# GpSimd's fills for the paired heads wait for step 24 instead of step 16, and the planner gets one weight instead of five

## The chip, the cores and the metric

The kernel runs on one core of a Trainium2 chip. The metric is the device time of one execution in microseconds, as a median over runs of the same program on the same chip. The profile shows one execution, taken by the hardware profiler.

The engines are named as in the profile: PE is the matrix engine (TensorE), PEld its weight loads, DVE is VectorE, ACT is ScalarE, POOL is GpSimd and SP is SyncE, which here issues nearly all of the DMAs. SPq, POOLq and the like are the sequencers of these engines.

## The reference

A causal attention with a decay runs over 4 batches, 8 heads, 576 positions and heads of 64. Its output, 2304 tokens by 512, goes through two MLPs (512 to 2048 to 512), the first with a squared ReLU, the second with a piecewise quadratic:

```python
scores = q @ k.T / sqrt(D) + cum[:, None] - cum[None, :]   # cum: running sum of log(clip(f))
attn = softmax(where(causal, -1e9, scores)); x = attn @ v  # per head, then heads side by side
h = x @ moe_w_in;   g = relu(h) ** 2;                               x = g @ moe_w_out
h = x @ moe2_w_in;  g = where(h >= 1, h, where(h <= -1, 0, (h + 1) ** 2 / 4));  out = g @ moe2_w_out
```

The weights are float64, the other inputs float32; the kernel computes each product of the MLPs as three float16 matmuls (high times high, low times high, high times low).

## The kernel before, in words

The tokens are cut into four blocks: blocks 0 to 2 have 512 columns each, the last one has 768. For each of the first three blocks the two MLPs run as 16 steps each (steps 0 to 15 of block 0's first MLP, 16 to 31 of its second MLP, 32 to 47 of block 1's first MLP, and so on). A step `s` has three parts: `h_group(s)` multiplies one 128-wide slice of the first weight matrix into a bank `h` (L1423 on PE, 12 matmuls); `act_group(s)` makes the activation `g` from it and splits it into a high half `gh` and a rest `gl` (in the second MLP L1451 and L1453 on ACT, L1455 on DVE, then L741 or L745 for `gh` and L758 for `gl`); `out_group(s)` multiplies `gh` and `gl` into the four accumulators `acc` (L1587 to L1589, 12 matmuls). `out_group(s)` follows one step behind, after `h_group(s + 2)`. The weights come in as float64 words (`raw`), are decoded (L1332, L1335 or L1336, L1340 or L1341, L1343), split (L1398 or L1399, L758) and stored for later use (L1405).

Attention is computed beside this: for positions below 256 in groups of four heads (`attention32`, tiles with a q in their name, such as `s6q`), and for the later positions in pairs of heads (`attention_pair`), first for block 2. The pairs need tiles that are partly constant: `Q1`, `Q2`, `K1`, `K2` (two of each, with zeros and with rows of plus or minus a constant), a wider `mask`, and a mask `pairs` for two heads at once. These constants are written once by POOL: `rows_of_pairs` makes 10 fills of Q tiles and 4 of K tiles (L668), one fill and one select for the mask (L653, L654), and one fill and two selects for `pairs` (L676, L678). All of them wait for one tiny POOL operation, the gate `gated<-x` (L662). In the kernel before it reads the last slice of `x2b[0]`, the input of block 0's second MLP, and the call is made at step 17.

After the fills, SP copies the decay rows into the tiles (`K<-cumhl`, `Q<-cumhl`, L1118), ACT and DVE write the heads' halves, and PE makes the first scores of a pair (L1141, L1142).

The order of all instructions on all engines is written out by a planner in the kernel file (`Schedule`). Every operation has a due time and a cost estimate, and where two engines can do it, one for each. `run` makes a list schedule and puts such an operation on the engine with the earliest weighted end, `(1 + weight) * cost` after its start, with weights for DVE and POOL and none for ACT. `improve` does that in seven rounds for each of the weights in `WEIGHTS`, with due times taken back from the round before, and keeps the plan that its own estimate finds shortest. In the planner, POOL and those DVE operations that are marked as sharing SBUF's port with it (a third entry in their cost) never overlap. Of the five weights of the kernel before, the plan that it runs is one of weight 0.6 for DVE and 0.3 for POOL.

Of the kernel before, what the change touches and what calls it, by code (L numbers as in the profile page):

```python
# [17 lines left out]
ALU = mybir.AluOpType  # L18
# [5 lines left out]
NKC = DM // P  # L24
NFC = DFF // P
# [41 lines left out]
def pattern(bits):  # L67
    return struct.unpack("f", struct.pack("I", bits))[0]
# [62 lines left out]
TURN = 0.05  # L131
LEAD = 15.4

WEIGHTS = [{"DVE": x, "POOL": x / 2} for x in (0.4, 0.5, 0.6, 0.8, 1.0)]

class Buf:
    def __init__(self, pool, make, kind=None):
# [25 lines left out]
class Schedule:  # L163
# [175 lines left out]
    def improve(self, pools, rounds):  # L339
        first = [o.due for o in self.ops]  # L340
        best = None
        for weight in WEIGHTS:
            for o, f in zip(self.ops, first):
# [71 lines left out]
def tile_attention_moe_moe(ctx: ExitStack, tc: tile.TileContext, qkv, f, w2, outT, halves, seen=None, bad=None):  # L415
# [19 lines left out]
    sch = Schedule()  # L435
# [111 lines left out]
    V = [T_START]  # L547
# [28 lines left out]
    gated = const.tile([1, 1], F16, name="gated")  # L576
# [13 lines left out]
    def setup():  # L590
# [3 lines left out]
        due = -100.0  # L594
        G, V_, A = nc.gpsimd, nc.vector, nc.scalar
# [56 lines left out]
        def triangle(a, z, due, deps=()):  # L652
            m1 = sch.op(due, {"POOL": ((z - a) / 1200 + 0.05, lambda: G.memset(mask[:, a:z], 0.0))}, deps)  # L653
            ms.append(sch.op(due, {"POOL": ((z - a) / 940 + 0.2, lambda: G.affine_select(  # L654
                out=mask[:, a:z], in_=mask[:, a:z], pattern=[[-1, z - a]], compare_op=ALU.is_ge,
                fill=-BIG, base=OFF - a, channel_multiplier=1))}, [m1]))
# [2 lines left out]

        def rows_of_pairs(due, x, ops):  # L660

            z = sch.op(due, {"POOL": (0.1, lambda: G.tensor_scalar(gated, x.tile[:1, 0, 1, :1], 1.0, None, op0=ALU.mult))}, ops, [x])  # L662
            gate = [z]
            for i in range(2):
                def fill(t, r, c, x, z):
                    bits = {0.0: 0, SQ: 0x78007800, -SQ: 0xF800F800}[x]
                    n = t[0:r, :, c].shape[2]
                    return sch.op(due, {"POOL": (n / 900 + 0.1, lambda: G.memset(t[0:r, :, c].bitcast(F32), pattern(bits)))}, [z])  # L668

                every, left, right = slice(0, None), slice(0, D), slice(D, None)  # L670
                z = fill(Q2[i], D, right, 0.0, gate[0])
                z = fill(Q2[i], 6, right, SQ, z)
                zs["Q", i] = [fill(Q1[i], P, left, 0.0, gate[0]), fill(Q2[i], P, left, 0.0, gate[0]), fill(Q2[i], 3, right, -SQ, z)]
                zs["K", i] = [fill(K2[i], 6, every, SQ, fill(K2[i], D, every, 0.0, gate[0]))]
            triangle(0, OFF + P - HEAD, due, gate)
            m1 = sch.op(due, {"POOL": (0.4, lambda: G.memset(pairs, 0.0))}, gate)  # L676
            for a in range(2):
                ms.append(sch.op(due, {"POOL": (0.5, lambda a=a: G.affine_select(  # L678
                    out=pairs[D * a:D * a + D, :], in_=pairs[D * a:D * a + D, :], pattern=[[-1, HEAD + D]],
                    compare_op=ALU.is_ge, fill=-BIG, base=HEAD, channel_multiplier=1))}, [m1]))  # L680

        if not halves:
            due = -30.0
            triangle(0, OFF + P - HEAD, 60)
            for i in range(2):
                for n, t in (("Q", Q2[i]), ("K", K2[i])):
                    z = None
                    for r, x in ((64, 0.0), (4, -1.0 if n == "Q" else 1.0)):
                        z = sch.op(due, {"POOL": (0.5, lambda t=t, r=r, x=x: G.memset(t[0:r, :].bitcast(F32), x))}, [z])
# [10 lines left out]
    cum_op, zs, mask_op, id_op, cumd_op, first_rows, rows_of_pairs = setup()  # L700
# [583 lines left out]
    def w_load(s):  # L1284

        if s >= NS:
            return
        first, again = {}, {}
        for layer, u in ((0, s + LAG), (1, s)):
            if 0 <= u < NS:  # L1290
                _, mo, fc = steps[u]
                pair = mo * NFC + (fc - LAG * (layer == 0)) % NFC
                (again if (pair, layer) in scr_op else first).setdefault(pair, []).append(layer)
        ops = whl_op[s] = []
        if first:
            b = new("raw" if halves else "big", f"raw{s}", [P, 2, 512], U64) if W64 else new("wf", f"wf{s}")
            loads = []
            for pair, layers in first.items():
                c = span(layers)
                size = P * (8 if W64 else 4) * 512 * len(layers)  # L1300
                loads.append(sch.op(V0(s + 2) - 17, {
                    "SP": (dma_t(size, late=2.5 if s < 0 else 0.0), lambda b=b, c=c, pair=pair: nc.sync.dma_start(
                        out=b.tile[:, c], in_=w2[pair].rearrange("p (l n) -> p l n", l=2)[:, c]))},
                    [], [b], early=RE[s + LAG] if s <= 0 else V0(s + 2) - 17 - LW))
                for layer in layers:
                    scr_op[pair, layer] = None
            raw[s] = b, loads
            new_pairs[s] = first
        if again:
            b = whl[s] = new("big", f"whl{s}")  # L1310
            for pair, layers in again.items():
                c = span(layers)
                ops.append(sch.op(V0(s + 2) - 7, {
                    "SP": (dma_t(P * 1024 * NB * len(layers), late=1.2), lambda b=b, c=c, pair=pair: nc.sync.dma_start(
                        out=wide(b.tile[:, c]), in_=scr[pair][:, c]))},
                    [scr_op[pair, layer] for layer in layers], [b]))
# [67 lines left out]
    def w_split(s):  # L1384

        if s not in wf:
            return
        c = span(sorted(layer for layers in new_pairs[s].values() for layer in layers))
        n = 512 * (c.stop - c.start)
        w = wf.pop(s)  # L1390
        if s not in whl:
            whl[s] = new("big", f"whl{s}")
        b = whl[s]
        due = V0(s + 2) - 4.5
        hi, lo = (lambda i=i: b.tile[:, c, i, :] for i in range(2))
        src, unit = lambda: w.tile[:, c], sw * (2.0 if W64 and not halves else 1.0)
        o = sch.op(due, {
            "ACT": (act_t(n), lambda: nc.scalar.activation(hi(), src(), AF.Copy, scale=unit)),  # L1398
            "DVE": (dve2_t(n), lambda: nc.vector.tensor_scalar(hi(), src(), unit, None, op0=ALU.mult), True),  # L1399
        }, whl_op[s], [w, b])  # L1400
        o = sch.op(due + 1, subs(lo, src, lambda: wide(hi()), n, scale=unit, seen=mark("w")), [o], [w, b])
        whl_op[s].append(o)
        for pair, layers in new_pairs[s].items():
            c_ = span(layers)
            store = sch.op(due + 6, {"SP": (dma_t(P * 1024 * NB * len(layers)), lambda c_=c_, pair=pair: nc.sync.dma_start(  # L1405
                out=scr[pair][:, c_], in_=wide(b.tile[:, c_])))}, [o], [b])
            for layer in layers:
                scr_op[pair, layer] = store


    h_op, gt, accs, acc_op, x2b, x2_op = {}, {}, {}, {}, {}, {}
# [210 lines left out]
    def attend(blk):  # L1622
        if blk:
            xb[blk] = new_x(f"x{blk}", blk)
        for g in groups:
            if g.blk == blk:
                attention32(g)
        if blk in carry:
            buf, (_, off, c0, c1), deps = carry[blk]
            n = c1 - c0  # L1630
            split_x(blk, range(NKC), off, lambda: buf.tile[:, :, :n], n, deps, buf, V[NFC * ATTENTION[blk][0]] + 2)
        for t in tasks:
            if t.blk == blk:
                (attention_pair if halves else attention)(t)
# [488 lines left out]
    for s in range(NS + LAG):  # L2123
        if s < NS:
            blk, mo, fc = steps[s]
            if halves and s == NFC + 1:
                rows_of_pairs(V[s] + 12, x2b[0], [x2_op[0, NKC - 1]])
            for b, (g, _) in ATTENTION.items():
                if s == NFC * g:
                    attend(b)  # L2130
            w_load(s + LAG)
            w_split(s)
            after = s >= NFC and steps[s - fc - 1] == (blk, 0, NFC - 1)
            if after and fc == 0:
                out_group(s - 2, V[s] - 3)
                out_group(s - 1, V[s] - 2)
            if not halved(s):
                h_group(s)
            elif fc % 2 == 0:
                pair_group(s)  # L2140
            w_decode(s + 1)
            in_sums(s)
            if not halved(s):
                act_group(s)
            if halves and blk in HALVED and fc == 1:
                half_sums(s)
        if s >= LAG and not (s < NS and after and fc < LAG):
            out_group(s - LAG, (V[s] + V[s + 1]) / 2)
# [86 lines left out]
```

## Time and profile before

| what | value |
|---|---|
| median of 3 runs | 863.54 us (862.9 to 866.13) |
| the profiled execution, its own time | 864.67 us |
| its span, first to last instruction | 862.8 us |
| PE busy | 845.9 us (98%) |
| DVE busy | 763.6 us (89%) |
| ACT busy | 605.3 us (70%) |
| POOL busy | 23.8 us (3%) |
| mean granted PE clock | 0.998 |

Busy time is time in which an engine has an instruction in work; a 128x512 matmul of float16 is shown with 0.38 us, but the next one starts 0.21 to 0.22 us after it, so that they overlap. What PE loses is read from the idle time that the timeline shows in brackets ahead of an instruction, together with what ended it.

### The profile page before, as it was taken

The numbers are of one execution on the slowest core, as the hardware profiler recorded it, in microseconds if no ns is written. First come the engines' busy times: TensorE is split into PE (matmuls) and PEld (weight loads), VectorE is DVE, ScalarE is ACT, GpSimd is POOL, SyncE is SP. The second block draws the span as 40 slices with busy tenths as digits, with TensorE's granted clock in tenths as the row PEclk, the third lists the DMA queues.
The fourth block names the chain that finished last, engine by engine and source line by source line (L and its number), as shares of the span: only waits on it lengthen the run. The fifth ranks groups of instructions, "written<-read, shape, count | busy, mean of one in ns | idle before, by whom it ended". The sixth has DMA issues, their size and how long they took to land.

```text
span 862.8 us, 14696 instructions
## 1 busy us (share of the span) xinstructions
PE 845.9 (98%) x4930; PEld 462.7 (54%) x4930; DVE 763.6 (89%) x1882; ACT 605.3 (70%) x1232; POOL 23.8 (3%) x120
## 2 busy tenths in 40 slices
PE   8999999999999999999999999999999999999996
PEld 7644444454444444444446654466556556665553
DVE  8999999999789878989888789986899998999993
ACT  7999988996677667767577577756564566756652
POOL 3000004000000000000000000000000000000000
PEclk9999999999999999999999999999999999999999
DMA  8799997886599998699489988677464454335432
GB/s 258 210 319 323 353 346 230 275 279 222 164 270 226 255 218 241 150 229 257 164 227 264 256 237 208 158 191 161 129 198 156 159 171 159 109 112 168 139 112 76
DMA packets 144841, 180.68 MB, mean 209 GB/s; under 512 B 91670, under 2 KB 96918, under 8 KB 140726
## 3 DMA queue, kind: packets, MB, share of 16 engines
q1 hardware_dynamic: 144750, 179.67, 71.2%
q8 instruction: 40, 0.66, 0.3%
q14 instruction: 43, 0.35, 0.1%
q10 hardware_dynamic: 8, 0.00, 0.0%
HBM read 127.84 MB, written 30.81 MB: 184 GB/s over the span
## 4 chain that ended last, share of the span: by engine, by line
PE 76%; DVE 12%; ACT 6%; DMA 3%; issue 2%; SPq 0%; POOL 0%; DVEq 0%; POOLq 0%; ACTq 0%
PE h L1423 17%; PE acc L1587 8%; PE acc L1589 8%; PE acc L1588 8%; PE h L1972 6%; PE av L1246 3%; PE X L1837 3%; PE Y L1837 2%; PE b L1924 2%; PE b L1926 2%; PE b L1925 2%; DVE wf L1343 2%; PE s L1147 1%; PE s L1146 1%; DMA PT<-PP 1%
## 5 line engine op out<-in xcount | busy, mean ns | idle before, releaser
L1423 PE MATMUL h<-x,whl 128*128 128x512 f16 x912 | 214.3, 379 | 1.0 <-DVE g L1455 1.0
L1423 PEld LDWEIGHTS <-whl 128*128 128x128 f16 x912 | 88.0, 98 | 103.5 <-issue 3.9
L1587 PE MATMUL acc<-gh,whl 128*128 128x512 f16 x312 | 118.3, 379 | 0.0
L1589 PE MATMUL acc<-gl,whl 128*128 128x512 f16 x312 | 118.2, 379 | 0.0
L1588 PE MATMUL acc<-gh,whl 128*128 128x512 f16 x312 | 118.2, 379 | 0.0
L1188 ACT ACTIVATE E<-E,st 128x448 f32<-128x448 f32 (+2 forms) x80 | 54.6, 682 | 33.2 <-DVE st L1186 17.7
L1222 DVE SCALAR_TENSOR_TENSOR PP<-E,st,PP 128x512 f16<-128x512 f32 (+2 forms) x112 | 62.0, 594 | 3.5 <-ACT PP L1218 3.1
L1218 ACT ACTIVATE PP<-E,st 128x512 f16<-128x512 f32 (+2 forms) x112 | 59.4, 588 | 5.9 <-issue 3.5
L1589 PEld LDWEIGHTS <-whl 128*128 128x128 f16 x384 | 37.6, 98 | 45.3
L758 DVE SCALAR_TENSOR_TENSOR gl<-g,gh 128x512 f16<-128x512 f32 x78 | 53.4, 686 | 8.1 <-PE acc L1589 3.2
L1587 PEld LDWEIGHTS <-whl 128*128 128x128 f16 x384 | 37.6, 98 | 40.0 <-issue 3.6
L1588 PEld LDWEIGHTS <-whl 128*128 128x128 f16 x384 | 37.6, 98 | 37.2
L764 DVE CUSTOM_DVE_ANT_0 E<-s,mask 128x288 f32<-128x288 f32 (+1 forms) x96 | 45.4, 509 | 12.1 <-PE s L1147 11.5
L1972 PEld LDWEIGHTS <-wi 128*128 128x128 f16 x336 | 32.9, 98 | 22.8 <-issue 0.9
L1451 ACT ACTIVATE r<-h,half 128x512 f32<-128x512 f32 x40 | 27.1, 678 | 23.6 <-PE h L1423 23.6
L1343 DVE SCALAR_TENSOR_TENSOR wf<-wf,low 128x1024 int32<-128x1024 int32 (+1 forms) x32 | 37.9, 1185 | 2.7 <-ACT low L1340 1.4
L758 DVE SCALAR_TENSOR_TENSOR whl<-wf,whl 128x1024 f16<-128x1024 f32 (+1 forms) x32 | 38.2, 1193 | 1.5 <-ACT whl L1398 1.4
L1332 ACT ACTIVATE wf<-raw 128x1024 f32<-128x1024 f32 (+1 forms) x32 | 35.8, 1119 | 2.0 <-DVE whl L758 1.9
L1641 DVE TENSOR_TENSOR G<-G 128x384 f32<-128x384 f32 x64 | 34.5, 552 | 0.8 <-ACT G L1988 0.4
L1972 PE MATMUL h<-x_last,wi 128*128 128x384 f16 x192 | 33.6, 326 | 0.7 <-DVE G L1996 0.7
L1441 ACT ACTIVATE r<-h 128x512 f32<-128x512 f32 x38 | 22.4, 589 | 13.5 <-PE h L1423 13.1
L1455 DVE SCALAR_TENSOR_TENSOR g<-r,h 128x512 f32<-128x512 f32 x40 | 27.2, 682 | 3.4 <-ACT r L1453 3.1
(620 smaller groups left out, 1924.8 us busy)
## 6 DMA issues: line engine op xcount, KB each, us to landing
raw<-in_w_dram SPq DMA_DIRECT2D x28, 1024.0 KB
whl<-scr SPq DMA_DIRECT2D x56, 512.0 KB
scr<-whl SPq DMA_DIRECT2D x28, 512.0 KB
wo<-scr SPq DMA_DIRECT2D x48, 256.0 KB
k<-in_qkv_dram SPq DMA_DIRECT2D x16, 576.0 KB
wi<-scr SPq DMA_DIRECT2D x23, 256.0 KB
q<-in_qkv_dram SPq DMA_DIRECT2D x16, 320.0 KB
v<-in_qkv_dram SPq DMA_DIRECT2D x16, 320.0 KB
```

Source lines behind the costliest of these rows:

```text
L758: nc.vector.scalar_tensor_tensor(out(), a(), scale, b(), op0=ALU.mult, op1=ALU.subtract, **kw)
L764: return nc.vector.tensor_tensor_reduce(out=out, in0=ps, in1=pairs[:, :n] if q0 is None else mask[:m, OFF - q0:OFF - q0 + n], scale=scale, ...
L1188: o_e.append(sch.op(dc + 0.5, {"ACT": (act_t(e, ptr=1) + 0.14, lambda a=a, e=e, at=at, Ec=Ec: nc.scalar.activation(Ec.tile[:, :e], Ec.tile ...
L1218: nc.scalar.activation(hi, x, AF.Copy, scale=r())
L1222: nc.vector.scalar_tensor_tensor(lo, x, r(), hi, op0=ALU.mult, op1=ALU.subtract)
L1343: return sch.op(due + 4.8, {"DVE": (dve_t(n) + 0.07, lambda: v.scalar_tensor_tensor(yi(), yi(), 3, part(), op0=ALU.logical_shift_left, op1 ...
L1423: nc.tensor.matmul(ps.tile[:, :n], w.tile[:, 0, wi, kc * P:(kc + 1) * P], src.tile[:, kc, xi, :n], start=(kc == 0 and i == 0), stop=(kc == ...
L1587: nc.tensor.matmul(a.tile[:, :n], wh, gh.tile[:, :n], start=(fc == 0), stop=False)
L1588: nc.tensor.matmul(a.tile[:, :n], wl, gh.tile[:, :n], start=False, stop=False)
L1589: nc.tensor.matmul(a.tile[:, :n], wh, gl.tile[:, :n], start=False, stop=(fc == NFC - 1))
L1837: nc.tensor.matmul(bank.tile[:, :n], wt(wi, kk), bt(xi, kk), start=start and z == 0, stop=z == len(todo) - 1, skip_group_check=not start)
L1972: nc.tensor.matmul(ps.tile[:, :n], W0.tile[:, j, wi, kc * P:(kc + 1) * P], src.tile[:, kc, xi, k * n:(k + 1) * n], start=(kc == 0 and i == ...
```

## The change

`rows_of_pairs` is called at step 25 (the tenth of block 0's second MLP) instead of step 17, with the due time of step 25 itself. Its gate reads one element of `gl` of step 24, and depends on the operation that makes that `gl`; before, it read the rest of block 0's `x2`. All fills and selects still wait for the gate. Beside this, `WEIGHTS` keeps the first of its five entries, so that the planner makes its seven rounds for DVE 0.4 and POOL 0.2 alone.

```diff
-WEIGHTS = [{"DVE": x, "POOL": x / 2} for x in (0.4, 0.5, 0.6, 0.8, 1.0)]
+WEIGHTS = [{"DVE": 0.4, "POOL": 0.2}]
...
         def rows_of_pairs(due, x, ops):
-            z = sch.op(due, {"POOL": (0.1, lambda: G.tensor_scalar(gated, x.tile[:1, 0, 1, :1], 1.0, None, op0=ALU.mult))}, ops, [x])
+            z = sch.op(due, {"POOL": (0.1, lambda: G.tensor_scalar(gated, x.tile[:1, :1], 1.0, None, op0=ALU.mult))}, ops, [x])
             gate = [z]
...
     for s in range(NS + LAG):
         if s < NS:
             blk, mo, fc = steps[s]
-            if halves and s == NFC + 1:
-                rows_of_pairs(V[s] + 12, x2b[0], [x2_op[0, NKC - 1]])
+            if halves and s == NFC + 9:
+                rows_of_pairs(V[s], gt[s - 1][1], [gt[s - 1][3]])
```

## Rows read from the trace of the kernel before

**Rows 1.** The page's first part: busy time, share and instructions of each engine.

```profile
PE 845.9 (98%) x4930; PEld 462.7 (54%) x4930; DVE 763.6 (89%) x1882; ACT 605.3 (70%) x1232; POOL 23.8 (3%) x120
```

**Rows 2.** Busy time by stage: stage, length, each engine's busy time, clock, DMA, GB/s.

```profile
40.00:140.00 100.00, 99.64 (x503) 49.60 (x503) 97.52 (x203) 91.06 (x175) 6.84 (x14) 1.00 0.95 316
140.00:220.00 80.00, 79.32 (x397) 38.36 (x396) 74.95 (x153) 65.11 (x112) 2.91 (x10) 1.00 0.77 255
```

**Rows 3.** Timeline of POOL, 130 to 145: start, length, instruction, count, idle before it.

```profile
132.99 0.21 POOL L662 TENSOR_SCALAR gated<-x 1x1 f16<-1x1 f16 x1 [125.42 <-DVE x L758]
133.13 1.24 POOL L668 MEMSET Q<- 64x320 f32 x5
134.33 2.38 POOL L668 MEMSET K<- 64x576 f32 x4
...
137.94 1.52 POOL L654 TENSOR_SCALAR_AFFINE_SELECT mask<-mask 128x384 bf16<-128x384 bf16 x1
...
140.94 1.41 POOL L668 MEMSET Q<- 64x320 f32 x5
```

**Rows 4.** Timeline of DVE, 132 to 147: four instructions during the fills, the activation behind them.

```profile
134.03 0.89 DVE L837 TENSOR_SCALAR st6q<-st6q 128x4 f32<-128x4 f32 x1
...
136.66 1.01 DVE L1336 TENSOR_SCALAR low<-raw 128x1024 uint16<-128x1024 uint32 x1
137.57 1.53 DVE L758 SCALAR_TENSOR_TENSOR whl<-wf,whl 128x1024 f16<-128x1024 f32 x1
...
139.04 1.03 DVE L1341 TENSOR_SCALAR low<-raw 128x1024 uint16<-128x1024 uint16 x1
139.97 0.66 DVE L1455 SCALAR_TENSOR_TENSOR g<-r,h 128x512 f32<-128x512 f32 x1
...
141.62 0.69 DVE L758 SCALAR_TENSOR_TENSOR gl<-g,gh 128x512 f16<-128x512 f32 x1
142.23 0.16 DVE L837 TENSOR_SCALAR st6q<-st6q 128x4 f32<-128x4 f32 x1
```

**Rows 5.** The same operations by group, DVE, 145 to 230: busy, mean ns, idle before.

```profile
L758 DVE SCALAR_TENSOR_TENSOR whl<-wf,whl 128x1024 f16<-128x1024 f32 x10 | 12.2, 1221 | 1.4 <-ACT whl L1398 1.4
L1341 DVE TENSOR_SCALAR low<-raw 128x1024 uint16<-128x1024 uint16 x5 | 3.8, 754 | 0.0
L1336 DVE TENSOR_SCALAR low<-raw 128x1024 uint16<-128x1024 uint32 x4 | 3.0, 750 | 0.0
```

**Rows 6.** Timeline of PE: every wait from 120 to 280.

```profile
140.68 2.10 PE L1423 MATMUL h<-x,whl 128*128 128x512 f16 x9 [1.04 <-DVE g L1455]
...
256.22 1.66 PE L1246 MATMUL av<-PT,vt 128*64 128x320 f16 x23 [0.25 <-DMA PT<-PP]
275.61 1.66 PE L1246 MATMUL av<-PT,vt 128*64 128x320 f16 x23 [0.53 <-DMA PT<-PP]
```

**Rows 7.** Timelines of DVE, PE and POOL: step 24's gl, its reader, first scores, a queued fill.

```profile
183.59 0.69 DVE L758 SCALAR_TENSOR_TENSOR gl<-g,gh 128x512 f16<-128x512 f32 x1
...
190.71 0.38 PE L1587 MATMUL acc<-gh,whl 128*128 128x512 f16 x1
...
219.47 0.30 PE L1141 MATMUL s<-K,Q 128*128 128x320 f16 x1
...
176.09 0.53 POOL L1183 MEMSET E<- 128x64 f32 x2 [23.05 <-PE tr7q L862]
```

**Rows 8.** Timeline of SP's queue, 184 to 194: the decay rows and what stands behind them.

```profile
187.56 0.28 SPq L1118 DMA_DIRECT2D K<-cumhl  x1
...
191.47 0.30 SPq L1118 DMA_DIRECT2D Q<-cumhl  x1
...
192.29 0.37 SPq L1314 DMA_DIRECT2D whl<-scr  x1
```

**Rows 9.** Groups of one decode operation on either engine, 40 to 140: busy, mean ns, idle.

```profile
L1335 ACT ACTIVATE low<-raw 128x1024 uint16<-128x1024 uint32 x6 | 8.2, 1374 | 1.4 <-DVE wf L1343 1.4
L1336 DVE TENSOR_SCALAR low<-raw 128x1024 uint16<-128x1024 uint32 x14 | 10.8, 768 | 0.2
```

**Rows 10.** Timeline of PE: waits near the start and from 778 to 815.

```profile
28.47 1.11 PE L819 MATMUL s3q<-QK 128*128 128x128 f32 x6 [1.36 <-DMA QK<-cumd]
...
782.20 0.65 PE L1837 MATMUL Y<-t_o,wi 128*128 128x384 f16 x3 [0.23 <-DVE c L1641]
791.31 0.65 PE L1837 MATMUL Y<-t_last,si 128*128 128x384 f16 x3 [0.94 <-DVE c L1641]
...
813.95 1.14 PE L1972 MATMUL h<-x_last,wi 128*128 128x384 f16 x6 [0.70 <-DVE G L1996]
```

## The prediction, made before the changed kernel ran

> **What bounds the kernel now.** I read the page's busy shares first, then the stages, then PE's waits one by one. PE is busy 845.9 us of a span of 862.8 [rows 1], so all of its idle time together is 16.9 us, and no reordering can give more than a part of that. The stage table says who is near to making PE wait. From 40 to 140 us three engines are full at once: PE 99.6, DVE 97.5 and ACT 91.1 of 100 us. From 140 to 220 the pressure falls: DVE has 80 - 74.95 = 5.05 us free [rows 2]. The granted clock is 1.00, its upper level, in both [rows 2], so the clock plays no part.
>
> The timeline of PE says where PE really waits. Between 120 and 280 us there are three waits: 1.04 us at 139.64, ended by a DVE activation, and 0.25 and 0.53 us for transposes of the first pairs [rows 6]. The first one lies at the seam between the two MLPs of block 0, in the middle of POOL's fills, and it is what this change touches.
>
> **The change, part by part: what it takes away.** The gate opens at 132.99 and the last fill ends at 140.94 + 1.41 = 142.35, so the 19 fills and selects take 9.36 us [rows 3]. In that time DVE is slow. Four instructions there have equals without POOL beside them: L837 took 0.89 against 0.16 us right after the fills [rows 4], L1336 1.01 against 0.75, L1341 1.03 against 0.75, the rest of `whl` 1.53 against 1.22 [rows 4, 5]. The lengthening is 0.73 + 0.26 + 0.28 + 0.31 = 1.58 us, all of it ahead of the activation `g` that starts at 139.97 and ends at 140.63 [rows 4]. PE waits for just that one: `h` of step 18 goes on at 140.68, after 1.04 us of idling that began at 139.64 [rows 6]. Without the lengthening `g` ends at about 140.63 - 1.58 = 139.05, before PE wants its bank. The wait goes: **-1.04 us**. Bounds: nothing (the planner, which keeps POOL and DVE's port operations apart in its own account, fills the freed time with other DVE work, and `g` comes no sooner) to the whole 1.04.
>
> **What it adds, at the new place.** In the trace of before, the `gl` of step 24 ends at 183.59 + 0.69 = 184.28 [rows 7]. The gate would open there, and 9.36 us of fills end at 193.6. Five things could be late:
>
> DVE is slowed there as it was before, by about 1.58 us. What is due next on PE is `out_group(24)`, which reads that `gl` at 190.71, 6.43 us after it was ready [rows 7], and at the seam there was no such distance. So 1.58 us is covered by 6.43 us, and DVE's free 5.05 us up to 220 [rows 2] take it up. Cost: 0. Without that cover it would be the 1.58.
>
> The rows on how POOL and DVE hinder each other bound this from above. The lengthening was 0.26 to 0.73 us for an instruction, and a `gl` beside plain fills took its usual 0.69 us [rows 4]. The Trainium skill ("SBUF — State Buffer", section "Who interferes with whom") calls the port pair that the two engines share an exclusive lock, on which the loser blocks for the whole instruction, not a split; it lets two-input vector instructions pass beside GpSimd work that only writes, and the 0.69 us agrees with that. If the lock fell so badly that DVE stood for all of 9.36 us, 9.36 - 6.43 = 2.93 us would reach PE; that is a rival below.
>
> The decay rows are copied into K and Q by SP at 187.56 and 191.47 [rows 8]. In the old order the K fills end 134.33 + 2.38 - 132.99 = 3.72 us after the gate [rows 3], so at 188.0, and SP's queue would hold for 0.4 us; if the K fills came last, until 193.6, for 6.0 us. Behind it in the queue stand loads of raw weights, a store and a reload of weights at 192.29 [rows 8], for the steps from 32 on, which begin after the first scores, over 27 us later. Cost: 0; uncovered, 0.4 to 6.0.
>
> The first scores of a pair run at 219.47 [rows 7], 25.9 us after the fills would end. Cost: 0.
>
> On POOL itself, fills of single E blocks that ran early in before (the last ones at 176.09 [rows 7]) now queue behind the gate; they belong to the chunks after those first scores. Cost: 0. The gate also holds one of two `gl` buffers until POOL has read it, 0.21 us [rows 3], while PE reads it until after 190.71. Cost: 0.
>
> **The weights.** This part reaches further than the gate. The kernel before runs a plan of weight 0.6, and the changed one can only have a plan of weight 0.4, so every choice between ACT and DVE, and with it the order on all engines, is made anew. A DVE operation of 0.77 us is charged 0.2 x 0.77 = 0.15 us less, so near ties go to DVE. That moves no PE work; it can only make or remove waits. From 40 to 140 one decode operation alone stands on ACT 6 times, at 1.37 us, and on DVE 14 times, at 0.77 us [rows 9]. DVE has 2.48 us free there [rows 2]. From the trace I can't say which way it falls, so I take 0, with bounds from PE's waits (below) on one side and from DVE's filling up on the other.
>
> **The sum.** 864.67 us is the profiled execution's own time, 1.87 more than its span. 864.67 - 1.04 = 863.63. The median of the runs is 863.54, 1.13 below the profiled one, so the same step gives 863.54 - 1.04 = 862.50. A measurement of this kernel can tell about 0.5%, 4.3 us, from no change: below 859.2 is faster, above 867.9 slower.
>
> **The rivals.**
>
> *The wait only moves.* DVE has been full since 40 us [rows 2], and 97.5% busy leaves a queue behind every late operation. If DVE is the real limit up to the seam, taking 1.58 us from it gives the planner room for other DVE work and the wait returns as another one of the same size: 863.5. For it: DVE and ACT are both full ahead of the seam. Against: up to 139.64 PE lost nothing to that; of the 0.36 us it was idle from 40 to 140, all lies in this wait [rows 2, 6].
>
> *DVE fills up: slower.* The mechanism is the lower charge on DVE from 40 to 140. Its room is 2.48 us [rows 2] plus the 1.58 us freed. Each operation that moves from ACT adds 0.77 us [rows 9], so from the sixth on (5 x 0.77 = 3.9) each costs PE some 0.77 us at the seam. Ten moved ones cost 5 x 0.77 = 3.9 us, 866.4 on top of the forecast's 862.5; twelve cost 5.4, 867.9. For it: the nearly full stage and the one-sided change of the weight. Against: a change of 0.15 us in the charge turns only near ties, and the planner counts DVE's queue.
>
> *The lock at the new place: slower.* 2.93 us as above, on 862.5: 865.4. It decides once DVE falls more than 6.43 us behind during the fills. Against: 1.58 us measured in the same 9 us at the seam [rows 4, 5].
>
> *The new plan happens to be better.* It can take PE's other waits too: 0.25 + 0.53 us [rows 6], 2 x 0.23 + 0.94 + 0.70 = 2.10 us from 778 to 815 (the wait of 0.23 occurs twice), and 1.36 us near the start [rows 10]. With the seam all of them are 1.04 + 0.78 + 2.10 + 1.36 = 5.28 us: 858.3; without the one near the start 859.6. For it: these waits depend on the order alone. Against: a plan from seven rounds must remove nearly all of them, and the planner preferred another weight.
>
> That the gate does not hold is hardly possible, since every fill depends on it.
>
> **How the numbers follow.** Forecast 862.5: 0.42, with a range of its own from 861 to 864.5. The wait only moves, 863.5: 0.18. DVE fills up, 865 to 870: 0.15, of which 0.10 above 867.9. The lock, 865.4: 0.05. A better plan, 857.5 to 860: 0.20, of which 0.14 below 859.2. So faster 0.14, slower 0.10, same 0.76. The range runs from 858.3, the price of the better plan, to 867.2, within the case of the full DVE; about 0.07 is left out below and 0.11 above.
>
> **What would show it.** In the profile of after: the gate at about 183, reading `gl`; L837, L1336, L1341 and `whl` at their usual lengths around 134 to 140; no PE wait for `g` at the seam; the lengthening at 184 to 194 instead, with no PE wait behind it; the first scores near 219. A PE wait for `gl` or `g` after 184 would prove the lock, more decode operations on DVE with PE waits between 40 and 140 the full DVE. The prediction is wrong if the time moves by more than 2 us with all of these in place: then the new plan did it somewhere else, and the table by stage will say where.

## The result and the profile after

The changed kernel took 872.15 us (median of 4 runs, 871.63 to 876.69), the kernel before 863.22 us beside it (4 runs): a ratio of 1.0107 [1.0085, 1.0130]. It is slower by some 9 us, beyond the upper end of the range. The profiled execution took 871.85 us with a span of 870.0 us, 7.2 us more than the span of before.

The page of after, first part, answers to [rows 1], and the stages to [rows 2] (columns as there):

```profile
PE 848.3 (98%) x4930; PEld 462.8 (53%) x4930; DVE 768.9 (88%) x1899; ACT 592.5 (68%) x1215; POOL 24.7 (3%) x120
```

```profile
40.00:140.00 100.00, 95.63 (x476) 46.99 (x474) 93.86 (x192) 84.11 (x164) 0.00 (x0) 0.98 0.90 303
140.00:220.00 80.00, 79.80 (x403) 39.13 (x402) 77.11 (x159) 65.19 (x122) 10.54 (x23) 1.00 0.76 249
```

PE lost 4 us of work in the first stage, where in before it was full, and nothing in the second, where the fills now run. DVE and ACT both became emptier in the first stage (97.5 to 93.9 and 91.1 to 84.1 us), so neither of them was overloaded there, and the granted clock has a dip (0.98 on average).

The timeline of PE from 57 to 67 us shows the place. Columns: start, length, instruction, count, in brackets the idle time ahead of it and what ended it.

```profile
57.71 0.94 PE L1423 MATMUL h<-x,whl 128*128 128x512 f16 x3
62.40 0.97 PE L819 MATMUL s5q<-QK 128*128 128x128 f32 x4 [3.75 <-DMA QK<-cumd]
63.17 3.76 PE L1423 MATMUL h<-x,whl 128*128 128x512 f16 x9
```

PE stands for 3.75 us before the first scores of attention group 5 (`s5q`), and the nine `h` matmuls behind them take 3.76 us. Nine such matmuls, behind the scores of group 4, took 2.11 us in the kernel before:

```profile
49.97 2.11 PE L1423 MATMUL h<-x,whl 128*128 128x512 f16 x9
```

The stretches of after in steps of 3 us (columns as in [rows 2]) say why:

```profile
57.00:60.00 3.00, 1.65 (x11) 0.84 (x8) 2.96 (x7) 2.63 (x9) 0.00 (x0) 1.00 0.95 302
60.00:63.00 3.00, 0.60 (x4) 0.60 (x5) 3.00 (x5) 1.04 (x1) 0.00 (x0) 1.00 0.79 317
63.00:66.00 3.00, 3.00 (x9) 1.07 (x8) 2.09 (x5) 0.00 (x0) 0.00 (x0) 0.51 1.05 277
66.00:69.00 3.00, 3.00 (x14) 1.29 (x13) 0.00 (x0) 2.00 (x4) 0.00 (x0) 0.92 0.72 273
```

The granted clock was 1.00 until PE had stood still; from 63 to 66 us it was 0.51, its lower level (1.2 GHz), and then it rose again. In this trace the wait is so paid for twice.

What PE waited for is in the chain of waits (start, length, what); below it stands SP's queue, first of after, then of before:

```profile
51.36 10.91 DMA QK<-cumd
```

```profile
43.31 0.33 SPq L1302 DMA_DIRECT2D raw<-in_w_dram  x1
44.38 0.33 SPq L1405 DMA_DIRECT2D scr<-whl  x1
47.99 0.33 SPq L1302 DMA_DIRECT2D raw<-in_w_dram  x1
48.41 0.53 SPq L780 DMA_DIRECT2D QK<-in_qkv_dram  x1
50.33 0.33 SPq L1405 DMA_DIRECT2D scr<-whl  x1
50.71 1.21 SPq L793 DMA_DIRECT2D QK<-cumd  x2
```

```profile
41.10 0.33 SPq L1302 DMA_DIRECT2D raw<-in_w_dram  x1
41.52 0.38 SPq L1405 DMA_DIRECT2D scr<-whl  x1
45.04 0.33 SPq L1302 DMA_DIRECT2D raw<-in_w_dram  x1
...
46.90 0.53 SPq L780 DMA_DIRECT2D QK<-in_qkv_dram  x1
47.66 0.39 SPq L1405 DMA_DIRECT2D scr<-whl  x1
48.11 1.19 SPq L793 DMA_DIRECT2D QK<-cumd  x2
```

The two copies `QK<-cumd` (4 KB each) bring the decay rows of group 5. In both kernels two loads of raw weights (1 MB each), two stores (512 KB each) and the load of the group's q and k (512 KB) were issued in the 7 to 7.4 us ahead of them. In before the copies' eight packets ran between 53.2 and 53.5 us, and `s5q` started at 55.15 without a wait: a slack of 1.6 us. In after four of the packets ran at 55.9 to 56.6 us, two at 60.4 and two at 61.4.

The following table compares whole executions. It lists how much later than in before a given matmul of L1589 starts (its number counted from the start; four of them for each step), from the timelines of PE. e1 to e10 are the experiments below.

| L1589 no. (before, us) | after | e1 | e10 | e4 | e2 | e3 | e5 | e6 | e9 | e7 | e8 |
|---|---|---|---|---|---|---|---|---|---|---|---|
| 1 (46.50) | +3.21 | -0.48 | -0.86 | -0.45 | +2.02 | +2.06 | +2.44 | +2.07 | +1.75 | -0.54 | +5.71 |
| 8 (54.61) | +2.23 | -0.48 | -0.86 | -0.45 | +1.04 | +1.08 | +1.46 | +1.09 | +0.77 | -0.55 | +4.09 |
| 12 (60.81) | +8.33 | -0.47 | -0.86 | -0.44 | +7.09 | +8.05 | +8.74 | +2.76 | +1.28 | +2.59 | +9.02 |
| 64 (132.78) | +8.04 | -0.47 | -0.83 | -0.39 | +6.81 | +8.14 | +8.46 | +2.48 | +1.19 | +2.34 | +8.74 |
| 80 (164.31) | +7.20 | -1.67 | -2.03 | -1.36 | +6.29 | +6.94 | +7.61 | +1.68 | +0.60 | +2.87 | +8.36 |
| 128 (234.06) | +7.20 | -1.67 | -2.03 | -1.14 | +7.42 | +6.94 | +8.52 | +1.68 | +0.60 | +2.87 | +8.84 |
| 256 (435.71) | +5.62 | -1.65 | -2.04 | -2.72 | +6.12 | +5.40 | +6.93 | +0.10 | -0.99 | +3.09 | +7.26 |
| 288 (484.67) | +7.05 | -1.60 | -1.74 | +1.73 | +7.63 | +7.65 | +8.24 | +1.37 | +0.69 | +3.04 | +6.80 |
| end (862.79) | +7.20 | -1.65 | -1.83 | +0.84 | +7.64 | +7.92 | +8.44 | +1.20 | +2.17 | +2.74 | +7.01 |

In after, 2.2 us are lost before no. 8, and 6.1 us between no. 8 and no. 12, which is the place just shown. At the seam (no. 64 to 80) it wins 0.84 us; at the new place of the fills (no. 80 to 128) it loses nothing. In e5, which is the same kernel in another execution, 0.9 us go there; the experiment e5 below comes back to this.

What the prediction said to look for at the seam and behind it came as said in this trace. The timeline of DVE in after at the seam answers to [rows 4], that of PE there to [rows 6], and that of POOL at the new place to [rows 3]:

```profile
144.44 0.75 DVE L1336 TENSOR_SCALAR low<-raw 128x1024 uint16<-128x1024 uint32 x1
...
146.94 0.75 DVE L1341 TENSOR_SCALAR low<-raw 128x1024 uint16<-128x1024 uint16 x1
147.58 0.68 DVE L1455 SCALAR_TENSOR_TENSOR g<-r,h 128x512 f32<-128x512 f32 x1
```

```profile
147.89 2.10 PE L1423 MATMUL h<-x,whl 128*128 128x512 f16 x9 [0.20 <-ACT pr6q L741]
```

```profile
191.46 1.11 POOL L662 TENSOR_SCALAR gated<-gl 1x1 f16<-1x1 f16 x1 [184.29 <-DVE gl L758]
...
201.80 0.24 POOL L668 MEMSET Q<- 128x64 f32 x2
```

L1336 and L1341 have their usual 0.75 us (L837, at 145.86, its 0.17); PE's wait at the seam is 0.20 us instead of 1.04, and it is ended by a copy of group 6 on ACT (`pr6q`), no longer by `g`. The gate opens 7.2 us after the 184.28 us that were foreseen, and 7.2 us is what the kernel is late by then. From the seam to 450 us the trace of PE has no wait of over 0.15 us.

### The profile page after: what moved, and what is told of

It is laid out like the page before. It is cut to its first block, busy times and chain, and to the rows that moved or that the text cites. A ratio compares the mean times of both kernels' runs of the same rounds, so it can differ in the third digit from the quotient of the medians.

```text
span 870.0 us, 14691 instructions
## 1 busy us (share of the span) xinstructions
PE 848.3 (98%) x4930; PEld 462.8 (53%) x4930; DVE 768.9 (88%) x1899; ACT 592.5 (68%) x1215; POOL 24.7 (3%) x120
## 4 chain that ended last, share of the span: by engine, by line
PE 67%; DVE 20%; ACT 5%; DMA 4%; issue 3%; SPq 0%; DVEq 0%; ACTq 0%
PE h L1423 18%; PE acc L1587 7%; PE acc L1589 7%; PE acc L1588 7%; PE h L1972 5%; PE av L1246 2%; DVE c L1641 2%; DVE G L1641 1%; PE s L1147 1%; PE s L1146 1%; PE b L1924 1%; PE b L1926 1%; PE b L1925 1%; DVE whl L758 1%; DMA QK<-cumd 1%
## 5 line engine op out<-in xcount | busy, mean ns | idle before, releaser
L1423 PE MATMUL h<-x,whl 128*128 128x512 f16 x912 | 216.5, 381 | 0.2 <-ACT pr6q L741 0.2
L1589 PE MATMUL acc<-gl,whl 128*128 128x512 f16 x312 | 118.2, 379 | 0.0
L758 DVE SCALAR_TENSOR_TENSOR gl<-g,gh 128x512 f16<-128x512 f32 x78 | 53.6, 687 | 18.0 <-PE acc L1589 11.9
L1589 PEld LDWEIGHTS <-whl 128*128 128x128 f16 x384 | 37.5, 98 | 45.3
L1837 PEld LDWEIGHTS <-si 128*128 128x128 f16 x216 | 21.1, 98 | 15.4 <-issue 1.7
```

The costliest lines, as they stand in the source:

```text
L758: nc.vector.scalar_tensor_tensor(out(), a(), scale, b(), op0=ALU.mult, op1=ALU.subtract, **kw)
L1423: nc.tensor.matmul(ps.tile[:, :n], w.tile[:, 0, wi, kc * P:(kc + 1) * P], src.tile[:, kc, xi, :n], start=(kc == 0 and i == 0), stop=(kc == ...
L1589: nc.tensor.matmul(a.tile[:, :n], wh, gl.tile[:, :n], start=False, stop=(fc == NFC - 1))
```

## The experiments

Two theories stood against each other. A: the order that the planner makes anew with its new weight costs the time; the gate itself is as harmless as foreseen. B: the gate and the fills at the new place cost it, if not by a visible wait, then through what the planner arranges around them. In kernels e1, e6, e7, e9 and e10 one line is added in the file, and the line numbers of their profiles are higher by one from there on.

**e1: the order of before, only the gate moved.** The planner runs with the old gate and the weight that before's plan has; then the fills are put behind the `gl` of step 24 and the gate reads it. Every other instruction stands where it stood in before.

```diff
+WEIGHTS = [{"DVE": 0.6, "POOL": 0.3}]
-... G.tensor_scalar(gated, x.tile[:1, 0, 1, :1], 1.0, None, op0=ALU.mult)
+... G.tensor_scalar(gated, gate_tile[0].tile[:1, :1], 1.0, None, op0=ALU.mult)
...
+for i, o in enumerate(sorted(moved, key=lambda o: (o.start, o.seq))):
+    o.start = behind.start + 1e-6 * (i + 1)
```

> The order of all engines is that of the kernel before, instruction for instruction; only the gate of GpSimd's fills reads the gl of step 24 instead of x2. Theory A (the loss is in the new order of all engines, the gate itself helps a little): the 1.04 us wait of the matrix engine at the seam goes, nothing comes near 184 to 194 us, and the time is about 862.2 us, 1.0 below before. Theory B (the fills at their new place cost, by the port or by late users): 3 us or more slower than before, up to the 872 of the changed kernel, with waits of the matrix engine behind 184 us.

Measured: 863.17 us against 864.58 for before, a ratio of 0.9979 [0.9964, 0.9995]. From 100 to 230 us PE has no wait of over 0.15 us. The timeline of DVE at the seam, of DVE at the new place, and of POOL there:

```profile
135.28 0.75 DVE L1337 TENSOR_SCALAR low<-raw 128x1024 uint16<-128x1024 uint32 x1
135.91 1.22 DVE L759 SCALAR_TENSOR_TENSOR whl<-wf,whl 128x1024 f16<-128x1024 f32 x1
...
137.05 0.77 DVE L1342 TENSOR_SCALAR low<-raw 128x1024 uint16<-128x1024 uint16 x1
137.69 0.68 DVE L1456 SCALAR_TENSOR_TENSOR g<-r,h 128x512 f32<-128x512 f32 x1
```

```profile
186.56 0.62 DVE L746 TENSOR_SCALAR gh<-g 128x512 f16<-128x512 f32 x1
187.29 0.69 DVE L759 SCALAR_TENSOR_TENSOR gl<-g,gh 128x512 f16<-128x512 f32 x1
...
189.12 1.43 DVE L1344 SCALAR_TENSOR_TENSOR wf<-wf,low 128x1024 int32<-128x1024 int32 x1
190.59 0.89 DVE L1342 TENSOR_SCALAR low<-raw 128x1024 uint16<-128x1024 uint16 x1
191.37 1.02 DVE L1337 TENSOR_SCALAR low<-raw 128x1024 uint16<-128x1024 uint32 x1
```

```profile
182.43 1.11 POOL L663 TENSOR_SCALAR gated<-gl 1x1 f16<-1x1 f16 x1 [175.06 <-DVE gl L759]
...
191.84 1.68 POOL L669 MEMSET Q<- 64x320 f32 x5
```

L1337, L1342 and `whl`, which were lengthened in [rows 4], are back at their usual lengths, L838 too (0.17 us at 133.58), and `g` starts at 137.69 instead of 139.97. In the table, e1 wins 1.20 us from no. 64 to no. 80, and nothing is lost behind it. At the new place `gh` takes 0.62 us instead of 0.42 to 0.43, `wf` 1.43 instead of 1.22, L1342 0.89 and L1337 1.02 instead of 0.75: 0.20 + 0.21 + 0.14 + 0.27 = 0.82 us, with no PE wait behind them. B falls, for this order.

**e2: the order of after, only the gate taken back.** The fills and the gate go back to the seam, the gate reads `x2b[0]`; all else stands as in after.

```diff
-... G.tensor_scalar(gated, x.tile[:1, :1], 1.0, None, op0=ALU.mult)
+... G.tensor_scalar(gated, x2b[0].tile[:1, 0, 1, :1], 1.0, None, op0=ALU.mult)
...
+for i, o in enumerate(sorted(moved, key=lambda o: (o.start, o.seq))):
+    o.start = x2_op[0, NKC - 1].start + 1e-6 * (i + 1)
```

> The order of all engines is that of the changed kernel, only the gate of the fills reads x2 again, at the seam between the MLPs. Theory A (the loss is in the new order): about 872 to 873 us, the slow-down stays, with the 3.75 us wait for the decay rows at 59 us still there and vector instructions lengthened at the seam. Theory B (the fills at the new place cost): back to 863 to 865 us.

Measured: 871.82 us, ratio 1.0075 [1.0045, 1.0105]. The slowness stays without the gate's move, and the wait in PE's timeline with it:

```profile
61.16 1.29 PE L819 MATMUL s5q<-QK 128*128 128x128 f32 x4 [3.69 <-DMA QK<-cumd]
```

With e1 this settles A against B. What the gate gains within after's order can't be told from the times (1.0075 lies within the interval of e5, the changed kernel again); in the profile e2 has PE waits of 0.52 us at 146.45 (after: 0.20) and 0.76 us at 181.99 (after: none).

**e3 and e4: each part of the change alone, with a new plan.** e3 is before with the weight 0.4 alone, e4 is after with the weight 0.6 alone.

```diff
 e3, in the kernel before:
-WEIGHTS = [{"DVE": x, "POOL": x / 2} for x in (0.4, 0.5, 0.6, 0.8, 1.0)]
+WEIGHTS = [{"DVE": 0.4, "POOL": 0.2}]
 e4, in the changed kernel:
-WEIGHTS = [{"DVE": 0.4, "POOL": 0.2}]
+WEIGHTS = [{"DVE": 0.6, "POOL": 0.3}]
```

> The kernel before with the weight list cut to 0.4 and the gate where it was, so that only the planner's weight changes. Theory A1 (weight 0.4 is to blame, whatever the gate): 868 us or more, with the same wait for the decay rows of group 5 near 59 us. Theory A2 (each new plan falls out differently by some us, and the weight is not the cause by itself): anywhere from 860 to 870 us, with other waits of the matrix engine than in the changed kernel.

> The changed kernel with the one weight 0.6 in place of 0.4, so that the gate is new and the weight that of the plan of before. Theory A1 (weight 0.4 is to blame): 861 to 864 us, no wait for the decay rows of group 5. Theory A2 (each new plan falls out differently): anywhere from 860 to 870 us, and its waits lie at other places than those of before, though the weight is the same.

Measured: e3 871.37 us, ratio 1.0067 [1.0043, 1.0092], with the same wait before `s5q`; e4 865.51 us, ratio 1.0008 [0.9991, 1.0025], without it. So a plan of weight 0.4 makes the loss without the gate's move. PE's timeline in e3:

```profile
61.26 1.62 PE L819 MATMUL s5q<-QK 128*128 128x128 f32 x4 [3.76 <-DMA QK<-cumd]
```

e4 also shows what a plan made anew can do later on: 2.72 us ahead of before at no. 256, it loses 4.45 us in the next 50 us, among others at this wait of PE:

```profile
448.98 0.61 PE L1514 MATMUL Y68p<-tsum,sp68p 128*128 128x256 f16 x4 [1.23 <-DMA sp68p<-in_sum]
```

**e5: the changed kernel once more**, beside the next four.

> The changed kernel as it is, to stand on the same chip as the three below: about 871 to 872 us, 0.7% to 1.1% above before, with the wait of 3.7 us for the decay rows of group 5 near 58 us and the lower clock behind it.

Measured: 871.57 us, ratio 1.0080 [1.0054, 1.0107]; in this execution the wait is 5.15 us, and the copies land 11.9 us after their issue instead of 10.9: the same kernel differs here by a microsecond from one execution to the next. It also differs at the new place of the fills. From no. 100 to no. 108 this execution loses 0.9 us around the transposes and products of attention group 7 (`tr7q`, `av7q`), with this wait among them:

```profile
208.02 1.25 PE L876 MATMUL av7q<-pr7q,vt7q 128*64 128x256 f32 x8 [0.20 <-ACT pr7q L741]
```

Ahead of that group's softmax and beside POOL's selects, DVE's `whl` and L1336 took 1.52 and 0.99 us, as in after, and a `wf` 1.51 instead of 1.22. But e2, which has no fills at this place, loses 1.1 us at the transposes of the same group too. Whether the fills have a part in it was not tested.

**e6: after, with the rows of group 5 issued earlier.** The two copies `QK<-cumd` go ahead of the second raw load, the load of q and k and the store; the rest of SP's queue and all other engines stand as in after.

```diff
+(load5,), rows5 = groups[5].moves
+at = sp[sp.index(load5) - 1].start      # sp: SP's operations in order
+for i, o in enumerate(rows5):
+    o.start = at - 1e-5 * (2 - i)
```

> The changed kernel with one thing moved: SP issues the two copies of the decay rows of group 5 (4 KB each) ahead of the raw weights, the group's q and k and a store, and not behind these 2 MB; all other engines keep the order. Theory C (the small copies stand behind a backlog of big transfers, and the wait with the half clock behind it is some 6 of the lost 8 us): no wait for the rows near 58 us, clock 1.00 from 60 to 80 us, time about 866 us. Theory D (the transfers as a whole are late there, so the group's q and k or another buffer are waited for instead): a wait of 2 to 4 us stays at the same place with another releaser, time 869 to 872 us.

Measured: 866.44 us, ratio 1.0035 [1.0019, 1.0051], against 1.0080 [1.0054, 1.0107] for after in the same comparison. SP's queue, PE's timeline and the stretch behind it:

```profile
43.66 1.17 SPq L793 DMA_DIRECT2D QK<-cumd  x2
```

```profile
58.52 0.89 PE L820 MATMUL s5q<-QK 128*128 128x128 f32 x4 [1.01 <-ACT wf L1333]
```

```profile
60.00:80.00 20.00, 20.00 (x105) 9.46 (x103) 19.36 (x41) 16.42 (x34) 0.00 (x0) 1.00 0.89 324
```

The copies' packets now run at 48.2 to 48.5 us, 4 to 5 us after their issue, the wait falls to 1.01 us and the clock stays at its upper level. Issuing 8 KB some 6 to 7 us earlier in one queue (43.66 against 49.94 in e5 and 50.71 in after) takes 5.1 us off the kernel (871.57 - 866.44). From no. 8 to no. 12 e6 loses 1.67 us where after loses 6.10 and e5 7.28. What still waits 1.01 us is put down to an ACT operation that PE doesn't need there; e9 below names the other candidate.

**e7: the order of before, with the same rows issued later.** The counterpart: in before's order the copies go behind the next raw load.

```diff
+at = sp[sp.index(rows5[1]) + 2].start
+for i, o in enumerate(rows5):
+    o.start = at + 1e-5 * (i + 1)
```

> The kernel before with the opposite move: SP issues the same two copies some 5 us later, behind a store of decay sums and the next raw weights; all other engines keep the order of before. Theory C: the matrix engine waits 2 to 4 us for the rows near 55 us, the clock falls behind it, and the time rises to 866 to 869 us. Theory D: the rows land in time or the wait is won back later, time within 1 us of before.

Measured: 867.38 us, ratio 1.0045 [1.0028, 1.0062]. SP's queue, PE's timeline, the stretch behind it:

```profile
52.99 1.19 SPq L793 DMA_DIRECT2D QK<-cumd  x2
```

```profile
57.71 0.89 PE L820 MATMUL s5q<-QK 128*128 128x128 f32 x4 [2.94 <-DMA QK<-cumd]
```

```profile
60.00:80.00 20.00, 20.00 (x105) 9.48 (x104) 17.50 (x40) 17.77 (x34) 0.00 (x0) 1.00 0.82 290
```

The same wait can be made in the good order by this one transfer: 2.59 + 0.55 = 3.1 us from no. 8 to no. 12, kept to the end. The wait shows as expected, the fall of the clock doesn't: it stays at 1.00, its upper level.

**e8: after with all five weights.** The planner may choose again, and its estimate prefers the plan of weight 1.0.

```diff
-WEIGHTS = [{"DVE": 0.4, "POOL": 0.2}]
+WEIGHTS = [{"DVE": x, "POOL": x / 2} for x in (0.4, 0.5, 0.6, 0.8, 1.0)]
```

> The changed kernel with the list of five weights put back, so that the planner may choose another plan than that of weight 0.4, with the gate at its new place. Theory A1 (the plan of weight 0.4 is what costs): 861 to 865 us, no wait for the rows of group 5. Theory A2 (a new plan falls out by chance): 860 to 870 us, with waits of its own.

Measured: 870.01 us, ratio 1.0067 [1.0047, 1.0087]. PE's timeline and the stretch behind:

```profile
63.13 1.62 PE L819 MATMUL s5q<-QK 128*128 128x128 f32 x4 [2.64 <-DMA QK<-in_qkv_dram]
```

```profile
63.00:66.00 3.00, 2.87 (x8) 1.69 (x9) 3.00 (x7) 0.00 (x0) 0.00 (x0) 0.51 0.97 304
```

So it is not the value 0.4 as such. Another weight, with less on DVE (749.6 us busy) instead of more, waits at the same place for the same group's data. What differs between good and bad plans is when these transfers land; of the plans run here only those of weight 0.6 had them in time. And the clock fell to its lower level here (0.51) after a wait of 2.64 us, shorter than e7's of 2.94.

**e9: after, with the load of q and k and the rows both ahead** of the raw load and the store.

```diff
-for i, o in enumerate(rows5):
-    o.start = at - 1e-5 * (2 - i)
+for i, o in enumerate([load5, *rows5]):
+    o.start = at - 1e-5 * (3 - i)
```

> The changed kernel with SP issuing the q and k of group 5 (512 KB) and then its decay rows ahead of the raw weights and the store; all other engines keep the order. In the run with the rows alone moved a wait of 1.01 us was left before the scores of group 5. Theory C (that rest is the group's q and k, behind the same backlog): no wait there, a further 1 us off, about 865.5 us. If the rest is something else (the raw weights, now behind the group's data, or a bank): the wait stays or moves to a weight, 866 to 868 us.

Measured: 866.79 us, ratio 1.0029 [1.0011, 1.0046]. No wait is left before `s5q`, and no. 8 to no. 12 loses only 0.5 us; so e6's last 1.01 us hung on the load of q and k:

```profile
57.06 0.88 PE L820 MATMUL s5q<-QK 128*128 128x128 f32 x4
```

In time e9 can't be told from e6: it is 1.5 us ahead at no. 12 and 1.0 us behind at the end.

**e10: e1 once more**, beside many runs of before.

> The order of before with the gate at step 24 once more, on this chip: 0.1% to 0.3% under before, about 862 us, with no wait at the seam. If its gain was chance: 863 to 864 us, the same as before.

Measured: 862.63 us (12 runs) against 863.91 for before (23 runs), ratio 0.9987 [0.9976, 0.9998]; from no. 64 to no. 80 it wins 1.20 us, as e1 did. This version is ahead of before by 0.1 to 0.2%, and so ahead of both kernels.

## Why the prediction was wrong

**The seam: right.** Foreseen -1.04 us; the timelines give -1.20 (e1 and e10), the medians -1.41 and -1.28. The wait went with the lengthening, so the rival in which it only moves is refuted for the pinned order. The sum of 1.58 us left out one instruction: L854, at 135.64, took 0.55 us in before and 0.35 in e1, which makes 1.78; counted from the first `x` of the seam, `g` starts 1.83 us earlier in e1. In after's own order the gain from no. 64 to no. 80 is 0.84, and this is not the gate's alone: with the old gate, e3 gains 1.20 us there and e2 0.52.

**The new place: right, with one execution open.** The lengthening was put at 1.58 us. It is 0.82 us in e1, and no wait of PE follows there, in e1 or in after; the 0.9 us that e5 loses behind the fills are open. The lock as a price of 2.93 us is refuted: the most that one instruction lost was 0.27 us in e1 and 0.30 in after (a `whl` of 1.52). The Trainium skill ("SBUF — State Buffer", section "Who interferes with whom") says that two-input vector instructions contend with GpSimd work that reads, not with work that only writes, and e1 agrees: `gl` beside plain fills took 0.69 us, `wf` beside the masks' selects, which read, 1.43 instead of 1.22. One row shows no such effect: a `whl` that began at 187.90 kept its 1.22 us though a select started during it. SP's queue, the first scores and the gate's buffer cost PE nothing in e1 and after, as said.

**The weights: the step that failed.** "So I take 0", with DVE's filling up as the only way for the new plan to be slower. The size was wrong, and so was the mechanism. L1336 ran 15 times on DVE instead of 14, and L1335 4 times on ACT instead of 6, from 40 to 140 us (groups of after, answering to [rows 9]), yet DVE's busy time there fell, from 97.5 to 93.9 us:

```profile
L1336 DVE TENSOR_SCALAR low<-raw 128x1024 uint16<-128x1024 uint32 x15 | 11.3, 753 | 0.1
L1335 ACT ACTIVATE low<-raw 128x1024 uint16<-128x1024 uint32 x4 | 5.4, 1360 | 0.0
```

Over the whole kernel DVE has 5.3 us more work than in before, and that is not what makes it late: e8 is late at the same place with 14 us less. In place of 0 stands +8.3 us up to no. 12 in after's trace: 2.2 us from the start of the program, and 6.1 us at group 5. Of the 6.1 us, 3.75 are the wait; the slower clock is an estimate of 1.65 us for the nine matmuls (3.76 - 2.11), and 0.7 us remain. Of these, some 0.5 are the order and no wait: e9 loses as much between the same two matmuls without a wait and with the clock at 1.00, for all six transposes `tr4q` stand behind no. 8 in after's order, and three of them ahead of it in before's. e6 shows the cause for most of it by taking the late transfer away, e7 by making it late in the good order. Later on after wins 1.6 us (no. 128 to 256), loses 1.4 again (no. 256 to 288), and this nearly cancels. The rival of the better plan was right in its parts only: of the waits that it would take, 1.36 us near the start [rows 10] and 0.25 + 0.53 us [rows 6] are gone in after's trace, and the one of 0.94 is 0.36; the new wait and the slower clock are larger than all of that. The wait near the start differs between executions of one order: it is 1.84 us in e5, the same kernel as after, and 0.29 in e1, which has before's order.

The flaw in the reasoning has a clear form. I wrote that the order on all engines is made anew, and then priced it on one. For SP's queue I asked what the moved fills would delay at 187 us, not which transfers of the existing queue have little slack. The trace of before could have shown it: the rows of group 5 land at 53.5 us behind 3.5 MB of other transfers and are wanted at 55.15. This shows where a new plan can lose, and not how much; with 1.6 us of slack there, it had to get a bound on the slow side from this path too, and a larger chance than the 0.10 that I gave.

**What stays open.** Why the copies took 10.9 us in after and some 5 us in before, behind the same two loads, two stores and load of q and k: the DMAs moved less per microsecond in the 3 us behind the issue (after first, then before; the last two columns are the DMAs' busy share and GB/s), and nothing was run to say why.

```profile
51.00:54.00 3.00, 3.00 (x15) 1.37 (x14) 3.00 (x6) 3.00 (x6) 0.00 (x0) 1.00 0.92 273
```

```profile
48.00:51.00 3.00, 3.00 (x16) 1.68 (x15) 2.93 (x9) 2.44 (x5) 0.00 (x0) 1.00 1.10 392
```

Not tested either are the 0.8 to 2.2 us that the kernels with after's order or a plan of weight 0.4 lose before no. 8, and so nothing shows which part of it belongs to the order; their first waits are for the first group's data, 2.01 us in after and 0.85 in e5, and for its softmax (0.61 and 0.70 us in both).

## What to carry to other kernels

When a kernel's order comes out of a planner, a change to one dependency and one parameter is two changes, and the second reaches everything: run the part alone with the order pinned (e1) before judging it, and give the plan made anew a bound from every queue. To get it, list the transfers that land shortly before they are used, with what stands ahead of each in its queue. A few KB that are wanted soon are better issued ahead of the megabytes in that queue than behind them: here this was worth 5 us.

## What the runs showed of the hardware

- Two copies of 4 KB behind megabytes on one queue landed 10.9 us after their issue, their eight packets spread over 5.6 us; issued ahead of 2 MB of the same transfers they landed within 5 us.
- TensorE's granted clock fell to its lower level (0.51 over 3 us) after a wait of 3.75 us in after and after one of 2.64 us in e8, but stayed at 1.00 after one of 2.94 us in e7. What decides isn't settled by these runs.
- POOL's work took longer at the new place: the one-element gate 1.11 us in after, e1 and e10 instead of 0.21, and the fills with it 10.6 to 11.1 us instead of 9.36 (spans on POOL are rough). In all three the gate began during a `wf` on DVE (in after 191.28 to 192.50) and ended 0.06 to 0.07 us behind it; that the one held up the other is not tested.
